# Loading the first values behind all four key units of the first head, in a decode-attention kernel that streams its caches

## The chip, the cores and the metric

One core of one Trainium2 chip runs the whole program. The metric is the device time of one execution in microseconds (us), as the median of several executions. "Ratio" is always the mean time of one kernel's runs over the mean of the other's in the same rounds, so it is not quite the ratio of the medians that stand beside it. Times inside a profile are counted from the start of its span, and the span is about 2 us shorter than the execution's device time (1275.8 against 1277.71 us for the kernel before).

Names used below: HBM is the chip's main memory and SBUF the core's own memory of 128 partitions; 16 DMA engines move data between them. PE (TensorE) does the matrix products and transposes, VectorE and ScalarE work element by element, and SyncE issues the large loads. A semaphore is a counter on which an engine waits. A load has *landed* on one DMA engine when that engine's part of it is there and has been counted; the first and last landing of a load, and the idle time of the DMA engines, are counted from the trace's semaphore events and packets, which no view prints. The *granted clock* is the TensorE clock that the profile shows as granted, as a share of full speed.

## The reference, cut to what matters

One new token attends to a long cache, and a small gated feed-forward block runs beside it.

```python
# A: 16 query heads, 8 key/value heads, 65536 cached positions, head size 256, bf16
xn     = layernorm(A_x)                                   # [1, 1, 448]
q      = (xn @ A_wq) -> 16 heads of 256
scores = einsum("bhqd,bhkd->bhqk", q, repeat(A_k_cache, 2)) * 256 ** -0.5
p      = softmax(scores)
o      = einsum("bhqk,bhkd->bhqd", p, repeat(A_v_cache, 2)) @ A_wo
# B: a gated feed-forward block on the same row (B_w_gate, B_w_up, B_w_down)
out    = A_x + o + B(xn)
```

The two caches are 2 x 268 MB. Everything else is 12 MB. So the kernel is a stream of 549 MB from HBM, with some work on each piece.

## The kernel before

The kernel cuts each of the 8 key heads into four **key units** of 8.39 MB (128 positions for each of the 128 partitions), and the values likewise. A unit lies in one of three SBUF buffers of 64 KB per partition: keys alternate between buffers 0 and 1, values use buffer 2 (only the last head's values use all three). All the large loads are issued by SyncE on one queue, in the order in which this code lists them; an entry of `need` is a semaphore wait that SyncE makes before it issues that load.

```python
U = 4            # key units per head
HALVED = (0, 2, 3, 4)     # key units that are loaded as two halves, each with its own wait

def k_item(u):
    need = [("FREE", u - 2)] if u >= 2 else ()         # PE has transposed all of unit u-2: its buffer is free
    if u >= 2 and u in HALVED:
        need = {0: [("FREEH", u - 2)], 1: need}         # half 0 waits only for the first half of unit u-2
    slot_item("k", u, u % 2, ..., need)

def v_item(t):
    slot_item("v", t, 2, None, [("VFREE", t - 1)] if t else [("QT",), ("R",), ("CONST",)])

item("wq", [(wq_area, flat_src(A_wq, WQN), "wq")])
for u in range(U - 1):
    k_item(u)            # key units 0, 1, 2
v_item(0)                # values 0: waits only for the query product and set-up work, long done by then
k_item(U - 1)            # key unit 3
k_item(U)                # key unit 4, the first of the second head
k_item(U + 1)
for t in range(1, NT):
    v_item(t)
    if t + U + 1 < NU:
        k_item(t + U + 1)
# [... the last values, the weights of block B and of the output projection ...]
```

On PE, a key unit is 8 sets of transposes (evicted by VectorE and ScalarE) and of query products. Values of unit t are multiplied in the middle of key unit t + 4, when the scores of their whole head are known and their softmax is done:

```python
def turn_K(u):
    t = u - U
    # [...]
    def block():
        pe_V(v, 0, True, True)       # waits for the load of values t, then 32 matmuls
        pe_tot(v)
        pe_V(v, 1, True, True)
        # [...]
    k_sets(u, range(0, CSETS), at)   # sets 0 to 3 of key unit u, then FREEH
    ghostly(block)()                 # values t, only when u >= 4
    k_sets(u, range(CSETS, SETS), at)   # sets 4 to 7, then FREE
```

So in the first head PE works on keys alone, and values 0 are first read in the middle of key unit 4.

## Time and profile before

| | before |
|---|---|
| median, lowest and highest of 6 runs | 1277.78 us, 1277.47 to 1278.56 |
| span of the profile | 1275.8 us |
| PE / VectorE / ScalarE busy | 75% / 45% / 34% |
| moved by DMA | 549.20 MB, mean 430 GB/s |
| chain that ended last | DMA 80%, PE 17% |

Two rows of the page's view of the span in 40 equal slices, kernel before. A digit 9 means that the 16 DMA engines were busy 90% of the slice or more; the second row is what they moved in each slice.

```profile
DMA  9999999999999999999999999999999999999998
GB/s 408 426 429 443 432 436 432 434 432 438 434 429 438 427 440 429 436 436 429 438 432 436 432 434 427 440 432 434 438 427 438 432 436 434 432 432 436 426 431 353
```

The engines are busy in every slice, at nearly one rate. The first slice (408 GB/s) has the start, the last one (353) the end. The landings in the trace give the rate of one unit: from values 1 (168.23 us) to values 2 (206.92 us) two units pass in 38.69 us, which is 19.35 us for 8.39 MB, or 433.6 GB/s. The Trainium skill, page "DMA: Bandwidth & Descriptors", section "Where 436 GB/s comes from", gives 435.2 GB/s as the ceiling of the ports into SBUF; this trace agrees with it within 1%.

The next three fences are about the first head, where the change is. First SyncE's timeline of the kernel before, when each load is issued: start, duration of the issuing, instruction, count. A merged row "x3" starts with its first and ends with its last instruction.

```profile
47.88 0.33 SPq L910 DMA_DIRECT2D ring<-in_A_k_cache_dram  x1
48.34 0.36 SPq L910 DMA_DIRECT2D ring<-in_A_v_cache_dram  x1
65.07 11.73 SPq L910 DMA_DIRECT2D ring<-in_A_k_cache_dram  x2
87.89 35.48 SPq L910 DMA_DIRECT2D ring<-in_A_k_cache_dram  x3
144.17 0.33 SPq L910 DMA_DIRECT2D ring<-in_A_v_cache_dram  x1
```

These are: the second half of key unit 2; values 0; the two halves of key unit 3 (65.07 and 76.47); the halves of key unit 4 and key unit 5 (87.89, 99.30, 123.04); values 1. Then three pieces of the chain of waits of the same kernel (start, us, what), each from the issue of a load to its landing:

```profile
2.12 49.74 DMA ring<-in_A_k_cache_dram
...
65.07 35.30 DMA ring<-in_A_k_cache_dram
...
144.17 24.06 DMA ring<-in_A_v_cache_dram
```

The half unit issued at 65.07 takes 35.30 us to land, at 100.37, although half a unit is 9.7 us of transfer: it waited in the queue behind the rest of key unit 2 and values 0. Issuing early is only a place in the queue. The Trainium skill says it on the page "DMA: Bandwidth & Descriptors", section "Queues, rings and completion order": each engine consumes its ring in order. The landings here agree: loads land in the order of issue. The 16 parts of one load land some 1.75 us apart, the first at 98.61 and the last at 100.37 for this half unit, and the next load's first part lands at 108.32.

What PE did at that time (start, us, instruction, in brackets the idle time before it and what ended it):

```profile
51.91 1.97 PE L420 MATMUL ps_t<-ident_f,ring 128*128 128x128 f32 x8 [3.97 <-DMA ring<-in_A_k_cache_dram]
...
100.42 1.09 PE L420 MATMUL ps_t<-ident_f,ring 128*128 128x128 f32 x8 [1.06 <-DMA ring<-in_A_k_cache_dram]
...
138.44 3.35 PE L420 MATMUL ps_o<-ring,p_sb 128*4 128x512 bf16 x32 [2.02 <-ACT p_sb L572]
```

PE starts key unit 1 at 51.91 when it lands, and waits 1.06 us for key unit 3. It first reads values 0 at 138.44, and what it waits for then is the softmax on ScalarE, not the values, which landed at 90.66. So values 0 come some 48 us before they are needed. That was the question behind the change.

### The profile page before, as it was taken

The page shows a single profiled execution, that of the slowest core. Times are in us where ns is not written, and L with a number is a line of the kernel's source. Part 1 is how long each engine was busy: PE and PEld are TensorE (multiplying, and loading weights), DVE is VectorE, ACT ScalarE, POOL GpSimd, SP SyncE. Part 2 cuts the span into 40 slices and gives each one's busy share as a digit, 9 for nine tenths or more (in the row PEclk, how much of TensorE's full clock was granted, in tenths as well). Part 3 has the DMA queues.
Part 4 walks back from the last instruction along what each step waited for, and adds up shares of the span by engine and source line. Part 5 has one row for each costly group of instructions (what it writes and reads, how often), then busy time and mean ns, then how long its engine had stood idle before and what let it go on. Part 6 is the DMA issues. An engine that isn't in the chain of part 4 may idle for free.

```text
span 1275.8 us, 23503 instructions
## 1 busy us (share of the span) xinstructions
PE 956.0 (75%) x9735; PEld 624.7 (49%) x9735; DVE 570.3 (45%) x1078; ACT 436.2 (34%) x655; POOL 8.0 (1%) x38
## 2 busy tenths in 40 slices
PE   3898988778777679767778776787777687677664
PEld 3676655445544455444455454454454454444321
DVE  4566554345444455343454344454444554444310
ACT  2455433244333334323333332343332333332300
POOL 2000000000000000000000000000000000000000
PEclk9899999899888899888898888898888998888886
DMA  9999999999999999999999999999999999999998
GB/s 408 426 429 443 432 436 432 434 432 438 434 429 438 427 440 429 436 436 429 438 432 436 432 434 427 440 432 434 438 427 438 432 436 434 432 432 436 426 431 353
DMA packets 12742, 549.20 MB, mean 430 GB/s; under 512 B 1335, under 2 KB 1978, under 8 KB 3386
## 3 DMA queue, kind: packets, MB, share of 16 engines
q1 hardware_dynamic: 12724, 549.03, 99.7%
q8 instruction: 8, 0.13, 0.0%
q14 instruction: 4, 0.03, 0.0%
q10 hardware_dynamic: 6, 0.00, 0.0%
HBM read 549.03 MB, written 0.00 MB: 430 GB/s over the span
## 4 chain that ended last, share of the span: by engine, by line
DMA 80%; PE 17%; issue 1%; ACT 1%; DVE 1%; SPq 0%; ACTq 0%; DVEq 0%
DMA ring<-in_A_v_cache_dram 68%; PE ps_o L420 12%; DMA ring<-in_A_k_cache_dram 7%; DMA kt_all<-in_A_wo_dram 3%; DMA ring<-in_A_wo_dram 2%; PE ps_t L420 2%; PE ps_q L420 1%; PE ps_m L420 1%; ACT kt_all L481 1%; SPq L910 0%; DVE kt_all L479 0%; ACT S_sb L562 0%; PE ps_s L420 0%; DVE kt_all L712 0%; DVE kt_all L815 0%
## 5 line engine op out<-in xcount | busy, mean ns | idle before, releaser
L420 PE MATMUL ps_t<-ident_f,ring 128*128 128x128 f32 x4096 | 586.6, 285 | 84.5 <-DMA ring<-in_A_k_cache_dram 61.6
L479 DVE COPY kt_all<-ps_t 128x1024 bf16<-128x1024 bf16 x768 | 487.0, 684 | 293.8 <-PE ps_q L420 289.0
L420 PEld LDWEIGHTS ps_t<-ident_f,ring 128*128 128x128 f32 x4096 | 450.2, 143 | 237.2 <-issue 135.2
L481 ACT ACTIVATE kt_all<-ps_t 128x1024 bf16<-128x1024 bf16 x256 | 262.0, 1023 | 508.4 <-PE ps_q L420 508.4
L420 PE MATMUL ps_o<-ring,p_sb 128*4 128x512 bf16 x2044 | 177.1, 508 | 204.6 <-DMA ring<-in_A_v_cache_dram 200.3
L420 PEld LDWEIGHTS ps_o<-ring,p_sb 128*4 128x4 bf16 x2044 | 53.0, 101 | 292.6 <-issue 264.2
L420 PE MATMUL ps_q<-kt_all,q_cur 128*2 128x512 bf16 x2056 | 164.9, 398 | 0.3 <-DVE kt_all L479 0.3
L503 ACT ACTIVATE s<-ps_q 98x512 bf16<-98x512 f32 x257 | 151.6, 590 | 1.3 <-PE ps_q L420 1.3
L585 DVE RECIPROCAL rs<-ps_m 128x4 f32<-128x4 f32 x29 | 5.3, 182 | 272.2 <-PE ps_m L420 272.2
L572 ACT ACTIVATE p_sb<-S_sb 128x128 bf16<-128x128 bf16 x64 | 18.9, 307 | 260.8 <-PE ps_o L420 260.6
L420 PEld LDWEIGHTS ps_s<-sel_bf,s 128*128 128x128 bf16 x1032 | 64.7, 98 | 5.3 <-ACT s L503 1.9
L420 PE MATMUL ps_s<-sel_bf,s 128*128 128x8 bf16 x1032 | 63.7, 167 | 1.3 <-ACT s L503 1.3
L628 DVE CAST ob_sb<-ps_o 100x512 bf16<-100x512 f32 x29 | 20.0, 691 | 89.9 <-PE ps_o L420 89.9
L420 PEld LDWEIGHTS ps_q<-kt_all,q_cur 128*2 128x2 bf16 x2056 | 26.4, 79 | 44.2 <-issue 44.2
L420 PEld LDWEIGHTS ps_m<-rowsum,ones_f 128*128 128x128 f32 x58 | 12.3, 264 | 22.6 <-issue 22.6
L481 ACT ACT_TABLE_LOAD x7 | 9.0, 1283 | 20.8 <-PE ps_q L420 20.8
L532 DVE TENSOR_REDUCE m1p<-S_sb (+1 forms) x33 | 13.9, 422 | 4.4
L420 PE MATMUL ps_m<-rowsum,ones_f 128*128 128x4 f32 x58 | 14.8, 326 | 0.0
L530 DVE CAST S_sb<-ps_s 128x256 f32 (+1 forms) x33 | 13.6, 413 | 1.9 <-PE ps_s L420 1.9
L562 ACT ACTIVATE S_sb<-S_sb,negmax 128x512 bf16<-128x512 bf16 x16 | 13.2, 851 | 3.2 <-DVE negmax L556 3.2
L420 PE MATMUL ps_m<-diag,ones_f 2*128 2x2 f32 x58 | 11.2, 260 | 3.6 <-DVE diag L547 0.6
L420 PEld LDWEIGHTS ps_m<-diag,ones_f 2*128 2x128 f32 x58 | 8.7, 187 | 10.5 <-DVE diag L547 10.5
(93 smaller groups left out, 128.3 us busy)
## 6 DMA issues: line engine op xcount, KB each, us to landing
ring<-in_A_k_cache_dram SPq DMA_DIRECT2D x8, 4096.0 KB, 30.5
ring<-in_A_v_cache_dram SPq DMA_DIRECT2D x1, 4096.0 KB, 27.3
ring<-in_A_wq_dram SPq DMA_DIRECT2D x1, 3584.0 KB, 11.5
ring<-in_A_wo_dram SPq DMA_DIRECT2D x1, 2688.0 KB, 28.7
ring<-in_A_v_cache_dram SPq DMA_DIRECT2D x1, 2048.0 KB, 31.8
ring<-in_B_w_gate_dram SPq DMA_DIRECT2D x1, 1568.0 KB, 16.5
ring<-in_B_w_up_dram SPq DMA_DIRECT2D x1, 1568.0 KB, 19.9
ring<-in_B_w_down_dram SPq DMA_DIRECT2D x1, 1568.0 KB
```

The source lines that it names most:

```text
L420: return pe.matmul(*a, **k)
L479: O(e, ("EV", s, m), lambda it: nc.vector.tensor_copy(out=kt[:, :], in_=tb[:, :]), f"ev{m}")
L481: O(e, ("EV", s, m), lambda it: nc.scalar.activation(out=kt[:, :], in_=tb[:, :], func=ACTF.Copy), f"ev{m}")
L503: O("act", ("EVQ", s), lambda it: nc.scalar.activation(out=s2[s % 2][0:QROWS, :], in_=ps_q[0:QROWS, :], func=ACTF.Copy), "evq")
L530: O("dve", ("SCOPY", u), lambda it: nc.vector.tensor_copy(out=S_sb[:, at(it, SBN), :], in_=ps_sn), "sc")
L532: O("dve", ("SMAX", u), lambda it: nc.vector.tensor_reduce(out=m1p[:, :, at(it, 1)], in_=S_sb[:, at(it, SBN), :].rearrange("p n i -> p i n ...
L562: O("act", ("EXP", h, i), lambda it, i=i: nc.scalar.activation(out=S_sb[:, :, i], in_=S_sb[:, :, i], func=ACTF.Exp, bias=negmax[:, i:i + 1 ...
L572: O("act", ("PC", t, c), lambda it: nc.scalar.activation(out=p_sb[:, c, :, :], in_=S_sb[:, n:n + CH, :], func=ACTF.Copy), "pc")
L585: O("dve", ("RS", t), lambda it: nc.vector.reciprocal(out=rs[:, :, :], in_=ps_m[0:P, C_TOT:C_TOT + NH * rep]))
L628: O("dve", ("OB", t), lambda it: nc.vector.tensor_copy(out=ob_sb[0:OROWS, :], in_=ps_o[0:OROWS, :]))
```

## The change

The intent: values 0 are not needed early, key unit 3 is needed and PE waits for it; so key unit 3 goes first.

```diff
     item("wq", [(wq_area, flat_src(A_wq, WQN), "wq")])
-    for u in range(U - 1):
+    for u in range(U):
         k_item(u)
     v_item(0)
-    k_item(U - 1)
     k_item(U)
     k_item(U + 1)
```

No instruction is added or removed. On SyncE one load changes places with two; the other engines' programs are the same.

## The prediction

> **What bounds the kernel now.** The DMA engines. The page's slices show them 90% busy or more in 39 of 40 slices. One 8.39 MB unit of keys or values takes 19.35 us (landings of successive units in the trace), that is 433 GB/s; 549 MB at that rate is 1267 us of the 1275.8 us span. The Trainium skill, page "DMA: Bandwidth & Descriptors", "Where 436 GB/s comes from", gives 435.2 GB/s as the ceiling of the ports into SBUF; the trace agrees within 1%. PE is busy 75%; the chain of waits is 80% DMA. So only idle time of the transfer queue, put in or taken out, can move the total.
>
> **What the change does.** No instruction is removed or added; only SyncE's order differs. All large loads share one in-order queue. Values 0 now stand behind key unit 3 and its two waits (PE having transposed the halves of key unit 1). Those waits were covered by the transfers of key unit 2 and values 0; now only by key unit 2's.
>
> **Ledger of the first head** (us from the start; issues from the SyncE timeline; landings are of the last of 16 engines, the first being about 1.75 us earlier):
>
> - Unchanged: the halves of key unit 2 land at 61.6 and 71.3 (first engine 69.5). PE frees the halves of key unit 1 at 65.07 and 76.47, when key unit 3 is issued today.
> - After: half 1 of key unit 3, issued 65.07, is queued 4.4 us before the first engine runs dry; it lands at about 81.0. Half 2, issued 76.47, has 2.8 us (dry at 79.2); it lands at 90.7. Values 0, issued at once behind it, land at 110.1 instead of 90.7; they are first read at 138.4, so nobody waits. Key unit 4, issued at 88 and 99.3 as today, lands at 119.8 and 129.5 as today: the bytes ahead of it are the same.
> - Is 2.8 us enough? Today's values 1 are issued at 144.17, 2.9 us before the first engine runs dry at 147.1; one engine of 16 idles there for about half a microsecond, and values 1 land at full rate. I expect a similar dent at about 79 us: 0 to 0.3 us.
> - Gain: PE no longer waits 1.06 us for key unit 3 at 100.4, so key unit 5 and values 1 are issued about 1 us earlier (122, 143) and the dent at 147 goes. Their transfers still start when the queue reaches them.
>
> From values 1 on both queues are the same, with margins of 10 us and more (values 2: issued 172.5, its turn at 187.8).
>
> **On the critical path:** only the two dents, both under 0.5 us. Predicted time 1277.8 us, 1276 to 1280 with 80%; faster by over 2% 0.01, within 2% 0.97, slower by over 2% 0.02.
>
> **What would show it.** Right: DMA share and GB/s of the first four slices as before; values 0 land near 110; key units 4 and 5 at 129.5 and 148.9 within 0.5 us; PE's wait before key unit 3 gone, PE's busy time unchanged. Wrong: a stretch from 70 to 90 us with DMA share under 0.95, and every later landing shifted by that loss.
>
> **What would make it wrong.** A lower granted TensorE clock during key unit 1 (0.66 was granted between 50 and 60 us in this trace) that frees its halves later: each us beyond the 2.8 costs a us at the end, for the full queue gives nothing back. Full clock there would free them about 1.8 us earlier (13.2 us for that half against 11.4). A chip whose transfers run at another rate moves both kernels alike.

## The result, and the profile after

| | before | after |
|---|---|---|
| median (lowest to highest), 6 runs each | 1277.78 (1277.47 to 1278.56) | 1278.60 (1277.38 to 1279.52) |
| ratio, 95% interval | | 1.0005 (0.9992 to 1.0018) |
| span of the profile | 1275.8 us | 1275.4 us |
| values 0 landed (first to last engine) | 88.90 to 90.66 | 108.18 to 110.17 |
| key unit 3, second half landed | 108.32 to 110.09 | 88.83 to 90.82 |
| key unit 4, second half landed | 127.75 to 129.51 | 127.60 to 129.60 |
| key unit 5 landed | 147.11 to 148.87 | 146.95 to 148.95 |
| values 1 landed | 166.47 to 168.23 | 166.31 to 168.29 |

The two kernels are the same within the noise. The same rows of the page, kernel after:

```profile
DMA  9999999999999999999999999999999999999998
GB/s 410 425 434 437 435 432 434 434 434 436 434 430 438 430 438 432 432 434 434 434 436 434 430 438 430 438 432 432 434 434 432 438 434 432 436 430 436 421 436 355
```

SyncE's timeline after:

```profile
47.97 28.19 SPq L909 DMA_DIRECT2D ring<-in_A_k_cache_dram  x3
76.29 0.35 SPq L909 DMA_DIRECT2D ring<-in_A_v_cache_dram  x1
87.25 34.57 SPq L909 DMA_DIRECT2D ring<-in_A_k_cache_dram  x3
142.56 0.33 SPq L909 DMA_DIRECT2D ring<-in_A_v_cache_dram  x1
```

Key unit 3 is issued at 64.42 and 75.84 (the last two of the first row), almost as before: the wait that holds it is for PE, and PE's work has not moved. Values 0 now come right behind. PE's timeline after, at the places shown of before:

```profile
51.91 1.36 PE L419 MATMUL ps_t<-ident_f,ring 128*128 128x128 f32 x8 [3.88 <-DMA ring<-in_A_k_cache_dram]
...
98.89 1.06 PE L419 MATMUL ps_t<-ident_f,ring 128*128 128x128 f32 x8 [0.18 <-ACT kt_all L480]
...
136.88 2.61 PE L419 MATMUL ps_o<-ring,p_sb 128*4 128x512 bf16 x32 [2.02 <-ACT p_sb L571]
```

PE's wait for key unit 3 is gone, and PE reaches values 0 at 136.88 instead of 138.44, 1.56 us earlier: 0.9 us of wait (1.06 less the 0.18 that are left), and a granted clock that stayed full a little longer (from 52 to 56 us its mean was 0.57, and 0.50 before), so that PE was through with key unit 1 0.64 us earlier. And then the chain of waits, after:

```profile
142.56 25.74 DMA ring<-in_A_v_cache_dram
```

Values 1 are issued 1.61 us earlier than before, their transfer takes 1.68 us longer, and they land at 168.29 where before they landed at 168.23. The gain on PE has become time in the queue.

### The profile page after: what moved, and what is told of

It reads as the page before. It is cut to its first block, busy times and chain, and to the rows that moved or that the text cites. A ratio compares the mean times of both kernels' runs of the same rounds, so it can differ in the third digit from the quotient of the medians.

```text
span 1275.4 us, 23503 instructions
## 1 busy us (share of the span) xinstructions
PE 961.5 (75%) x9735; PEld 627.7 (49%) x9735; DVE 571.0 (45%) x1078; ACT 436.2 (34%) x655; POOL 8.0 (1%) x38
## 4 chain that ended last, share of the span: by engine, by line
DMA 77%; PE 19%; ACT 2%; issue 1%; DVE 1%; SPq 0%; ACTq 0%; DVEq 0%
DMA ring<-in_A_v_cache_dram 68%; PE ps_o L419 13%; DMA ring<-in_A_k_cache_dram 4%; PE ps_t L419 3%; DMA kt_all<-in_A_wo_dram 3%; DMA ring<-in_A_wo_dram 2%; ACT kt_all L480 2%; PE ps_q L419 2%; PE ps_m L419 1%; SPq L909 0%; DVE kt_all L478 0%; ACT S_sb L561 0%; PE ps_s L419 0%; DVE kt_all L711 0%; DVE kt_all L814 0%
## 5 line engine op out<-in xcount | busy, mean ns | idle before, releaser
L419 PE MATMUL ps_o<-ring,p_sb 128*4 128x512 bf16 x2044 | 183.1, 521 | 206.2 <-DMA ring<-in_A_v_cache_dram 201.9
```

The lines of the kernel that those rows point to most:

```text
L419: return pe.matmul(*a, **k)
```

## The experiments

**Theory.** The time is set by a transfer queue that must never run dry. Where a load stands in it does not matter, as long as each following load is issued far enough ahead of the moment when the queue has drained. With values 0 behind key unit 3, the second half of key unit 3 is issued only 3.1 us before the first DMA engine lands the half ahead of it (75.84 against 78.97); this is enough. I call this time the margin of a load. **Rival 1:** the order does not matter at all here, because PE has slack later (75% busy) and gives back whatever the first head loses. **Rival 2:** the thin margin does cost something, near the 0.8 us between the medians.

The experiments make the margin bigger or smaller. To compare them I use, besides the times, the landing of values 1: in all these orders the same bytes stand ahead of it in the queue (wq, key units 0 to 5, values 0), so how late it lands is what the queue lost before it.

| run | values 1 landed, last engine | later than before (168.23) | median | over the median of before, same chip |
|---|---|---|---|---|
| after (first result) | 168.29 | 0.06 | 1278.60 | 0.82 |
| after_again | 168.29 | 0.06 | 1278.61 | 0.64 |
| after_more | 168.28 | 0.05 | 1277.80 | 0.02 |
| between | 168.15 | -0.08 | 1277.65 | -0.32 |
| between_more | 168.32 | 0.09 | 1277.57 | -0.21 |
| before_full | 168.19 | -0.04 | 1277.97 | 0.31 |
| late1 | 170.57 | 2.34 | 1279.83 | 1.86 |
| behind4 | 170.83 | 2.60 | 1281.32 | 3.66 |
| ahead2 | 172.08 | 3.85 | 1281.57 | 3.91 |
| after_full | 176.34 | 8.11 | 1286.65 | 8.68 |
| behind5 | 191.60 | 23.37 | 1302.47 | 24.81 |

### after_full: the changed order, and the margin taken away

```diff
-            need = {0: [("FREEH", u - 2)], 1: need}
+            need = {0: need if u == U - 1 else [("FREEH", u - 2)], 1: need}
```

Both halves of key unit 3 now wait until PE is through with all of key unit 1.

> The changed order, but both halves of key unit 3 wait until PE is through with all of key unit 1 (the first half is issued at about 76.3 instead of 64.4 us). My theory: the queue is dry from about 69.5 to 71 until 78 us; 7.5 to 10 us lost, none given back: 1285.3 to 1287.8. Rival (PE has slack later and gives it back): within 1 us of 1277.8.

Measured: 1286.65 us (1286.22 to 1287.33), ratio 1.0067 (1.0053 to 1.0080). Key unit 3 was issued at 76.87. The stretches of 10 us of this kernel (us, busy time and instructions of PE, PE's weight loads, VectorE, ScalarE, Pool, then granted clock, DMA share, GB/s; a packet is counted where it starts, so a share can be over 1):

```profile
60.00:70.00 10.00, 9.65 (x100) 6.96 (x100) 7.22 (x14) 4.89 (x7) 0.00 (x0) 1.00 0.90 390
70.00:80.00 10.00, 9.56 (x101) 7.26 (x98) 6.83 (x11) 5.71 (x8) 0.00 (x0) 1.00 0.27 92
80.00:90.00 10.00, 9.65 (x100) 6.95 (x100) 7.22 (x14) 4.97 (x8) 0.00 (x0) 1.00 1.00 433
```

The queue is dry from about 70 to 78 us (all 16 engines are idle from 71 to 77), while PE is as busy as ever (9.56 of 10 us). The 8.1 us that values 1 land later are all in the time at the end. PE had 25% of slack over the whole run and gave nothing back: Rival 1 falls.

### before_full: the same later wait, in the order of before

The same one-line edit, on the kernel before.

> The order of before with the same later wait: both halves of key unit 3 wait for all of key unit 1. Here values 0 stand in front of them and fill the queue until about 90 us. My theory: issued at 76.4, in the queue 12 us before its turn, no engine idle, lands at 100.4 and 110 as in before: 1277.5 to 1278.5. Rival (a later wait costs the same wherever values 0 stand): 7.5 to 10 us longer, as the same edit in the changed order.

Measured: 1277.97 us (1277.62 to 1278.63), ratio 1.0002 (0.9988 to 1.0015). Key unit 3 was issued at 76.65, as late as in the last experiment, and the same stretch reads:

```profile
70.00:80.00 10.00, 9.56 (x99) 7.32 (x99) 7.04 (x12) 5.92 (x8) 0.00 (x0) 1.00 0.97 419
```

One edit, two prices: 8.7 us where key unit 3 stands right behind key unit 2, nothing where values 0 stand in front of it. This is what the place of values 0 did in the kernel before: they are a load that waits for nothing, and they covered the two waits of key unit 3. The change gives this cover away, and does not need it.

### late1: the changed order, and only the second half issued one set of transposes later

```diff
-            need = {0: [("FREEH", u - 2)], 1: need}
+            need = {0: [("FREEH", u - 2)], 1: [("T", 2 * SETS, TORD[-1])] if u == U - 1 else need}
```

> The changed order, but the second half of key unit 3 waits for one more set of transposes on PE (issued at about 79.1 instead of 76.3 us). My theory: no margin left, the engines run dry for 0.9 us (last engine) to 2.9 us (first engine) near 79 to 81 us, all later landings move by that, and the time is longer by the same 0.9 to 2.9 us: 1278.7 to 1280.7. Rival (later slack gives it back): 1277.8.

Measured: 1279.83 us (1278.75 to 1280.51), ratio 1.0012 (0.9999 to 1.0026). The second half of key unit 3 was issued at 78.67 instead of 75.84, 2.8 us later, and values 1 landed 2.34 us later. So the changed kernel stands near the edge: its margin is about one set of transposes. A stretch of 8 us where the two differ, first late1 and then the kernel after:

```profile
76.00:84.00 8.00, 7.83 (x79) 5.76 (x80) 5.86 (x12) 4.04 (x7) 0.00 (x0) 1.00 0.92 348
```

```profile
76.00:84.00 8.00, 7.76 (x79) 5.73 (x79) 5.87 (x12) 4.05 (x7) 0.00 (x0) 1.00 1.01 430
```

The rate fell more than the busy share. The parts of 32 KB that came first after the dry spot were slow: the ten that started between 79.6 and 79.9 us took 1.67 to 2.07 us in late1, where parts started between 79 and 80 us in the kernel after took a median of 1.21 us. Why is not shown.

### behind4: values 0 one unit further back, behind key unit 4

```diff
-    for u in range(U):
+    for u in range(U + 1):
         k_item(u)
     v_item(0)
-    k_item(U)
     k_item(U + 1)
```

> Values 0 one unit further back, behind both halves of key unit 4. My theory: the halves of key unit 4 are issued at 87.3 and 98.7 us with 1.7 us and about 0 us before the first engine runs dry; 1 to 3.5 us lost, values 0 land at about 131 and are not waited for: 1278.8 to 1281.3. Rival (order does not matter as long as values 0 land before they are read at 136): 1277.8.

Measured: 1281.32 us (1280.54 to 1282.83), ratio 1.0029 (1.0014 to 1.0045), at the upper edge of what was expected. Values 0 landed at 132.09, before PE read them. Values 1 landed 2.60 us later than before, within the expectation. Two stretches of it:

```profile
85.00:95.00 10.00, 9.65 (x101) 6.89 (x100) 6.18 (x11) 4.63 (x8) 0.00 (x0) 1.00 1.01 396
95.00:105.00 10.00, 9.56 (x100) 7.33 (x99) 7.09 (x12) 6.05 (x9) 0.00 (x0) 1.00 0.96 374
```

The first half of key unit 4 was issued at 87.29, 1.71 us before the first engine landed the half ahead of it (89.00), so the queue was not yet empty. Still its last part landed at 102.30, which is 11.57 us after the last part of the load ahead, where half a unit takes 9.71 us in a full queue: 1.86 us lost. So a margin can be above zero and yet too small.

The profiled run was 1280.95 us, 3.24 us over the profiled run of before, about 0.6 us more than the 2.60 explain. The rest arose at the end of the kernel: at 1264.78 the last engine was 3.28 us behind the first, the same late lag as in after_again (see the section on "between" below).

### behind5: values 0 behind key unit 5

```diff
-    for u in range(U):
+    for u in range(U + 2):
         k_item(u)
     v_item(0)
-    k_item(U)
-    k_item(U + 1)
```

> Values 0 behind key unit 5, so values 0 and values 1 stand next to each other in the queue. My theory: key unit 5 is issued at 121.5 while the queue ran dry at about 111 (about 12 us lost); values 0 land at about 162, PE waits some 25 us for them; values 1 need the same buffer, are issued at about 168, another 8 us dry. About 20 us longer: 1294 to 1302. Rival (slack later gives it back): under 1285.

Measured: 1302.47 us (1301.51 to 1303.70), ratio 1.0195 (1.0179 to 1.0211; the interval holds 2%, so by the 2% rule the verdict is unclear), 0.5 us above the range: I had left out the loss at key unit 4 that behind4 shows. Four stretches of it:

```profile
110.00:120.00 10.00, 9.56 (x99) 7.15 (x97) 6.87 (x12) 5.37 (x8) 0.00 (x0) 1.00 0.02 10
...
140.00:150.00 10.00, 0.00 (x0) 0.00 (x0) 0.00 (x0) 0.00 (x0) 0.00 (x0) 0.50 1.07 465
150.00:160.00 10.00, 0.00 (x0) 0.00 (x0) 0.00 (x0) 0.00 (x0) 0.00 (x0) 0.50 1.01 439
160.00:170.00 10.00, 6.59 (x70) 2.60 (x71) 0.48 (x2) 0.60 (x2) 0.00 (x0) 0.59 0.08 33
```

The two kinds of idle time stand here side by side. From 110 to 120 the queue is dry and PE works; that is lost. From 140 to 160 PE stands still, waiting for values 0, and the queue is full; that in itself loses nothing. But because PE stood still, values 1 could not be issued (they need the buffer of values 0), and from 162 to 170 the queue is dry again. Here the wait of PE cost only through the load that it delayed.

### ahead2: values 0 one place further forward, ahead of key unit 2

```diff
-    for u in range(U):
+    for u in range(U - 2):
         k_item(u)
     v_item(0)
-    k_item(U)
-    k_item(U + 1)
+    for u in range(U - 2, U + 2):
+        k_item(u)
```

> Values 0 one place further forward, ahead of key unit 2. My theory: the queue is full with values 0 until 71.3, key unit 2 lands at 81 and 90.7, so PE waits 4 to 5 us for it at 76 and frees key unit 3 that much later, at 127 to 129; key unit 5 is then issued at the moment the queue runs dry: 0.5 to 3 us lost, 1278.3 to 1280.8. Rival (earlier values are never worse): 1277.8.

Measured: 1281.57 us (1280.84 to 1282.22), ratio 1.0027 (1.0012 to 1.0042). The direction was right, the size too small. The place where it lost first was the expected one: key unit 2 landed at 80.98, PE waited 5.21 us for it, and key unit 5 was issued at 129.04. What I had missed is a second dry spot: PE took from 129.04 to 150.11 to get through half of key unit 4 and values 0 (21.1 us, as in the kernel before, from 123.04 to 144.17), so values 1 were issued at 150.11, when key unit 5 was landing (150.15 to 151.13). Of the 3.85 us, 2.26 were lost before key unit 5 and 1.59 before values 1. Stretches of ahead2, then of the kernel before:

```profile
125.00:130.00 5.00, 4.74 (x51) 3.86 (x48) 3.77 (x6) 3.02 (x4) 0.00 (x0) 1.00 0.49 210
...
145.00:150.00 5.00, 5.00 (x63) 1.77 (x51) 0.18 (x1) 0.38 (x2) 0.00 (x0) 0.66 0.91 393
150.00:155.00 5.00, 4.92 (x53) 3.58 (x50) 2.98 (x5) 2.24 (x4) 0.00 (x0) 1.00 1.09 419
```

```profile
125.00:130.00 5.00, 3.63 (x40) 2.90 (x39) 2.76 (x5) 3.76 (x5) 0.00 (x0) 1.00 1.19 513
...
145.00:150.00 5.00, 4.82 (x52) 3.47 (x51) 3.22 (x6) 2.85 (x4) 0.00 (x0) 1.00 1.01 433
150.00:155.00 5.00, 4.91 (x54) 3.56 (x53) 3.12 (x6) 2.20 (x4) 0.00 (x0) 1.00 1.00 433
```

Values 0 too early cost as much as too late, by another way: they make PE wait for keys, and PE is what issues the later loads.

### between, and the changed kernel twice more: does the thin margin cost anything?

Values 0 between the two halves of key unit 3, so that the second half has values 0 in front of it (in the changed kernel):

```diff
         for k, (sem, J) in enumerate(parts or [("slot%d" % s, SBN)]):
+            if (kd, u, k) == ("k", U - 1, 1):
+                v_item(0)
 # ...
-    v_item(0)
     k_item(U)
```

On one chip with late1 and after_full:

> The changed kernel once more, five rounds, to size the difference. My theory (queue always full, the second half of key unit 3 issued 2.8 us before the first engine runs dry): within 0.3 us of before when the granted clock is full in key unit 1, up to 1 us longer in single runs where it is not; ratio 0.9995 to 1.0010, with a wider spread of runs than before has. Rival (the place of values 0 does not matter at all, later slack absorbs anything): ratio 1.0000 and the same spread as before.

> Values 0 between the two halves of key unit 3. The thin margin (second half issued at 76.3, 2.8 us ahead) becomes over 20 us, only the first half's 4.4 us margin is left. If the thin margin is what makes the changed kernel's median 0.8 us longer, this one goes back to before: 1277.5 to 1278.0, spread as before. If the 0.8 us is chance, both have medians within 0.5 us of before. Key unit 3's second half lands at 110, PE waits for it less than 0.5 us.

Measured: after_again 1278.61 us (1277.59 to 1279.19), ratio 1.0002 (0.9988 to 1.0015); between 1277.65 us (1277.30 to 1278.25), ratio 0.9996 (0.9983 to 1.0010), the second half of key unit 3 landing at 110.04 and PE not waiting for it. That looked like a price of the margin, so both were run once more on another chip:

> The changed kernel a third time, next to the kernel with values 0 between the halves, on one chip. So far the changed kernel's medians are 1278.60 and 1278.61, between's 1277.65, before's 1277.7 to 1278.0. If the thin margin costs anything, the median is again 1278.3 to 1278.9 and at least 0.4 us above the next run's. If it was chance, the two medians are within 0.4 us.

> If the thin margin costs anything: 1277.4 to 1278.0 and under the changed kernel's median by at least 0.4 us. If it was chance: within 0.4 us of it, wherever that lies.

Measured: after_more 1277.80 us (1277.56 to 1279.57), ratio 1.0006 (0.9992 to 1.0019); between_more 1277.57 us (1277.38 to 1277.94), ratio 1.0000 (0.9986 to 1.0014). By the expectation (medians at least 0.4 us apart) this is a vote for chance: 0.23 us. Yet the 16 runs of the changed kernel reach from 1277.38 to 1279.57 us, with a mean of 1278.40, and the 10 of between only from 1277.30 to 1278.25, with a mean of 1277.64. The mean differs by 0.75 us or 0.06%, and it comes from runs of the changed kernel that are 1 to 2 us longer than its others. Over 1278.2 us lie 10 of the 16 runs of the changed kernel, 1 of the 10 of between, and 7 of all 33 runs of the kernel before (1279.06 twice and 1279.13 among them; their mean is 1277.90). So the longer runs are more frequent in the changed order, as far as runs on several chips can be put together.

The traces show one thing that fits and one that doesn't. What fits: in the trace of after_again, a run of 1278.61 us, the granted clock in key unit 1 was lower (0.78 between 48 and 52 us, where the trace of the first result has 1.00), the second half of key unit 3 was issued at 76.64 instead of 75.84, and in the microsecond at 79 the engines were idle for 1.6 us summed over the 16. The traces of the two short runs (1277.38 and 1277.56 us) have no such dent. What does not fit: in all three, values 1 land at 168.28 or 168.29, and the last values that still have the regular rhythm at 1174.5. The long run lost its 1.3 us of span (1276.7 against 1275.4) later: about 0.5 us by 1232, and 0.8 us after 1251. There one engine fell back, so that at the landing at 1262.43 the last engine was 3.28 us behind the first, where it is 2.2 us in the trace of the first result. A 16 KB packet of the instruction queue, which lasts 1.08 us, lies just there, at 1257.99. All traces have that packet; whether it moves the end would depend on whether it meets an engine that is already late. The trace does not name the engine of a packet, so this stays a guess. So a cost of some 0.5 us on average for the changed order is likely by the counts, and under a tenth of a per cent; that the thin margin causes it is not shown. Against it speaks that the dent at 79 us left no trace in the landing of values 1, and that the long run lost its time at the end.

No version beats the kernel before by more than the noise: between is 0.04% faster in one call and equal in the other, inside both intervals. While the queue is full, nothing was won by the order of loads in the first head. The last slice, at 353 GB/s, may leave something; no run tried it.

## Why the prediction was right

- *What bounds the kernel.* Right. Nearly every microsecond in which the queue was dry appeared in the time (8.1 us of late landing, 8.7 us of time in after_full; 3.85 and 3.9 in ahead2), and a microsecond of PE waiting did not (1.06 us taken away by the change).
- *What moves.* Right, to a few tenths: values 0 were predicted to land at 110.1 and landed at 110.17; key unit 4 at 129.5 and 129.60; key unit 5 at 148.9 and 148.95; key unit 5 and values 1 were to be issued at 122 and 143, and were at 121.49 and 142.56.
- *The margin of 2.8 us at the second half of key unit 3 is enough.* Right: the profiled run had 3.1 us, because the granted clock in key unit 1 was higher than in the trace that the prediction used, and has no dent at 79 us. after_again, at a lower clock, had 2.3 us, less than predicted, and a dent of 1.6 us over 16 engines, 0.1 us each, which is in the 0 to 0.3 us predicted; its values 1 landed at the same time. So it was not the luck of a fast clock. late1 shows that 2.8 us less than in the profiled run is not enough.
- *Each microsecond beyond the margin costs one at the end.* Right in after_full and ahead2, within 0.6 us; in before_full nothing was lost and the time was the same. late1 sharpens it: its engines were idle for only 0.6 us each, but values 1 landed 2.34 us later, so the loss at a dry spot is more than the idle time. In behind4 the time grew by about 1 us more than the queue lost (3.66 against 2.60); where that comes from was seen (the end of the kernel), not settled.
- *The total.* 1277.8 us predicted, 1278.60 measured, in the range. The 0.8 us is within the interval of the ratio. Over all calls the means differ by 0.5 us (16 runs of the changed kernel against 33 of before), a size that the prediction had not foreseen and whose cause stays open.
- *PE's busy time unchanged.* 956.0 before and 961.5 us after, with the same 9735 matmuls; the granted clock was 0.897 and 0.887. No effect of it shows in the landings.

## What to carry to other kernels

In a kernel whose transfer queue is full, do not ask only when a piece of data is needed, but how long before the queue drains the next load is issued; here a load that waits for nothing was worth most in front of one that waits. Work out that margin for each place from two numbers of the trace: when the load is issued (its buffer comes free), and when the first engine lands its part of the load ahead. Above zero is not enough. In the twelve traces every large load of the regular part with a margin from 2.34 us (after_again) to 6 us had its last landing where a full queue puts it, within 0.01 us: 9.71 us after the load ahead for half a unit, 19.35 for a unit. With the six margins from 1.71 us down to 0.03, the last landing was 0.7 to 2.4 us late (1.86 at 1.71 in behind4, 2.43 at 0.58 in late1). Where the margin was large enough, the new order moved no landing behind the reordered loads by more than 0.1 us, and a wait of PE, the busiest compute engine, that went away only became time in the queue.

## What the Trainium skill lacked or had wrong

- Page "DMA: Bandwidth & Descriptors", section "Latency and other measured facts", gives about 600 ns from issue to first byte for loads from SyncE, without saying from where it counts. Onto a dry queue (after_full, issued at 76.87) the first engine's packet starts 0.95 us after the start of the issuing instruction, which is 0.62 us after its end, and the sixteenth's 1.52 us after the start. So the figure fits the first engine, counted from the end; the 0.57 us between the engines is what it lacks.
- The same page says nothing of what a dry queue costs beyond its idle time. In after_full the first part of 32 KB of each engine after the dry spot took 1.61 to 1.97 us, the next ones 1.21. In late1 values 1 landed 2.34 us later although the engines were idle only about 0.6 us each (9.8 us over 16 engines from 78 to 82 us).
- The same page names two engines that are usually slower, but does not tell that the 16 engines stay apart for most of the run: in the kernel before, the first is 1.76 us ahead of the last at 61.59 us and still 1.61 us at 1174.45, while after the dry spot of after_full it is 0.63 us (at 89.05). So a margin counts from the first and the end from the last.
- Page "Runtime: NRT & Kernel Launch" says that instruction memory is refilled in blocks of 16 KiB; no page has how long one such packet lasts: 0.96 to 1.08 us each, 8 times in the changed kernel. What it takes from the data was not shown.
